# Decoding float64 weights in four passes in place of six, and moving three pairs of them to another stage

## The chip, the cores and the metric

The kernel runs on one core of a Trainium2 chip. The metric is device time in microseconds (us) of one execution; lower is better. TensorE does the matmuls, VectorE, ScalarE and GpSimd the elementwise work, and SyncE's queue issues nearly all DMAs. In rows of the profile these are PE (PEld is its weight load), DVE, ACT, POOL and SP.

## The reference

Three steps follow one another. First causal attention with a decay, for 4 batches x 8 heads, 576 positions, head size 64:

```python
scores = scale * (q @ k.T)
decay = cum[:, :, :, None] - cum[:, :, None, :]      # cum = cumsum(log(clip(f)))
attn = softmax(where(causal, -1e9, scores + decay))
x = (attn @ v) rearranged to [2304, 512]
h = x @ w_in                                         # 512 -> 2048
x = (h * sigmoid(h)) @ w_out                         # 2048 -> 512
out = ((x @ w_a) * (x @ w_b)) @ w_out2               # 512 -> 1536 -> 512
```

The weights `w_in`, `w_out`, `w_a`, `w_b`, `w_out2` arrive as float64, and the kernel has to make float32 numbers of them itself.

## The kernel before

**Stages.** In order of time: attention by pairs of heads (to about 183 us of the profiled span); the first in stage, `stage_in(0, ...)` (to about 361); the first out stage, `out_first` (to about 562), which begins with a part D of eight steps; the second in stage, `stage_in(1, ...)` (to about 827); the second out stage, `out_pairs`. Every matrix product is done by a Strassen-Winograd scheme: seven products of half-size blocks, on sums and differences of blocks that are called forms. Each float32 operand is split in a rounded part and a remainder (`split`: ScalarE casts, VectorE or GpSimd subtracts), and each product is three matmul passes. An in stage is a list `seq` of jobs (unit `u` of the weights, group `g` of tokens), seven products each.

**Weights.** They lie in 68 pieces of 128 x 512 numbers: 16 for the first in stage, 16 for its out stage (`F1`), 24 and 12 for the second. `decode(piece, ...)` fetches one piece (512 KB of float64) into a tile `raw` and makes float32 of it (L662 to L689). `load_unit` decodes the two pieces of one unit and makes the forms and their splits in one of three weight tiles `wA`, `wB`, `wC`. `load_piece` does the same for a piece of the first out stage, writes the decoded piece to DRAM (`wdram`) as well, and splits it into the tiles of `upper(v)`, two pieces for each of the eight `v`. `load_sums` later fetches the pair from `wdram` (`load_quarters`, into a tile of the tag `raw`) and makes the sums and differences that the other groups of tokens need. `decode_out(1, n)` decodes the 12 pieces of the second out stage during the second in stage and sends them to `wdram`.

**Tiles.** `raw`, `m` and `e` have two tiles each; tiles of one tag are given out in the order in which the program names them. Before the change the decoded piece is the tile `e`, and it is held until the unit's splits have read it; `raw` and `m` are free again at the end of the decoding.

**Order.** Nothing waits in a hand-written order. The class `Plan` simulates the engines with a cost for each operation, and at every step takes the ready operation that can start first; among those within 30 ns the one with the lowest priority number (`pr`, for most operations 1000 plus the planned time in us). An operation that may go to two engines (`either`: GpSimd or VectorE) gets the one that would end first. The order that comes out is each engine's program.

Of the kernel before, what the change touches and what calls it, by code (L numbers as in the profile page):

```python
# [9 lines left out]
F32 = mybir.dt.float32  # L10
F32R = mybir.dt.float32r
U32 = mybir.dt.uint32
BF16 = mybir.dt.bfloat16
AF = mybir.ActivationFunctionType
ALU = mybir.AluOpType
# [3 lines left out]
P = 128  # L19
# [20 lines left out]
PIECE = 512  # L40
# [4 lines left out]
UP = 5  # L45
# [179 lines left out]
def piece_of(stage, part):  # L225

    firsts = 2 * U1 + F1
    return {(0, "in"): 0, (0, "out"): 2 * U1, (1, "in"): firsts, (1, "out"): firsts + 2 * U2}[stage, part]
# [3 lines left out]
def model_kernel(ctx: ExitStack, tc: tile.TileContext, qk, q0, v, f, w, out):  # L232
# [44 lines left out]
    def buf(pool, tag, shape, dtype, name):  # L277
        n = SLOTS[tag]
        return Buf(tags[tag], lambda: (pools[tag] if pool is None else pool).tile(shape, dtype, name=name, tag=tag, bufs=n))
# [320 lines left out]
    def act(n, fn, reads, writes, prio):  # L600
        plan.add("ACT", 190 + n / 1.2, fn, reads, writes, prio)
# [2 lines left out]
        plan.add("DVE", 100 + n / 0.88 if sbuf else 165 + n / 0.96, lambda: fn(nc.vector), reads, writes, prio, port=sbuf)  # L604

    def pool(n, fn, reads, writes, prio):
        plan.add("POOL", 240 + 2.2 * n, lambda: fn(nc.gpsimd), reads, writes, prio)

    def either(n, fn, reads, writes, prio):
        plan.add("POOL", 240 + 2.2 * n, lambda: fn(nc.gpsimd), reads, writes, prio,  # L610
                 also=[("DVE", 100 + n / 0.88, lambda: fn(nc.vector))], port=True)

    def ss(n, fn, reads, writes, prio):
# [47 lines left out]
    def decode(piece, after, pr, single=False):  # L661

        n = PIECE
        if single:
            all_ = buf(zp, "z", [P, 3 * n], F32, f"raw_{piece}")
            raw, m, e = ((all_, i) for i in range(3))
            u = {raw: lambda: all_()[:, :2 * n].bitcast(U32), m: lambda: all_()[:, 2 * n:].bitcast(U32),
                 e: lambda: all_()[:, :2 * n].bitcast(U32).rearrange("p (c t) -> p c t", t=2)[:, :, 1]}
            ek = [e]
        else:  # L670
            raw = buf(dcp, "raw", [P, 2 * n], F32, f"raw_{piece}")
            m, e = (buf(dcp, t, [P, n], F32, f"{t}_{piece}") for t in "me")
            u = {t: lambda t=t: t().bitcast(U32) for t in (raw, m, e)}
            ek = [(e, 0), (e, 1)]
        src = w[piece * P * n:(piece + 1) * P * n].rearrange("(p c) -> p c", p=P)
        f = lambda t: u[t]().bitcast(F32)
        low, high = ((lambda k=k: u[raw]().rearrange("p (c t) -> p c t", t=2)[:, :, k]) for k in range(2))
        plan.dma(480, 8 * P * n, lambda: nc.sync.dma_start(u[raw](), src.bitcast(U32)), after, [raw], pr)
        act(n, lambda: nc.scalar.activation(f(m), high().bitcast(F32), AF.Copy, scale=2.0 ** -112), [raw], [m], pr)  # L679
        plan.add("DVE", 420, lambda: nc.vector.tensor_scalar(u[m](), u[m](), 3, None, ALU.logical_shift_left), (), [m], pr, port=True)  # L680
        plan.add("DVE", 690, lambda: nc.vector.scalar_tensor_tensor(  # L681
            u[m](), high(), 0x80000000, u[m](), ALU.bitwise_and, ALU.bitwise_or), [raw], [m], pr, port=True)
        plan.add("DVE", 600 if single else 420, lambda: nc.vector.tensor_scalar(u[e](), u[m](), 0xFF800000, None, ALU.bitwise_and), [m], ek + [raw] * single, pr, port=True)
        plan.add("DVE", 690, lambda: nc.vector.scalar_tensor_tensor(f(e), low(), 2.0 ** -52, f(e), ALU.mult, ALU.mult), [raw], ek, pr, port=True)  # L684
        if single:
            pool(n, lambda g: g.tensor_add(f(m), f(m), f(e)), ek, [m], pr)
            return m, lambda: f(m)
        pool(n, lambda g: g.tensor_add(e(), m(), e()), [m], ek, pr)  # L688
        return e  # L689

    def load_unit(stage, n, pr, after=()):

# [149 lines left out]
    def upper(v):  # L842

        t, n = (wouts[0][0], v) if v < UP else (wouts[0][1], v - UP)
        return t, lambda: t()[:, n * 2048:(n + 1) * 2048].rearrange("p (i f c) -> p i f c", i=2, f=4)
# [19 lines left out]
    def split_keys(n, hi, lo, val, reads, keys, pr):  # L865

        act(n, lambda: nc.scalar.copy(hi(), val()), reads, [k + (0,) for k in keys], pr)
        either(n, lambda e: e.tensor_sub(lo(), val(), hi().bitcast(F32)), list(reads) + [k + (0,) for k in keys], [k + (1,) for k in keys], pr)

    def load_piece(n, p):  # L870

        v, j = n // 2, n % 2
        t, w = upper(v)
        e = decode(piece_of(0, "out") + n, (), p)
        ek = [(e, 0), (e, 1)]
        plan.dma(480, 4 * P * PIECE, lambda: nc.sync.dma_start(wdram[0][n], e()), ek, [("w", 0, n)], p)
        split_keys(4 * P, lambda: w()[:, 0, 2 * j:2 * j + 2], lambda: w()[:, 1, 2 * j:2 * j + 2], lambda: e().rearrange("p (i c) -> p i c", i=2), ek,
                   [(t, v, 2 * j), (t, v, 2 * j + 1)], p)

    def load_sums(v, p, q):  # L880

        t, w = upper(v)
        low, x = lower(v)
        m, keys, combine = load_quarters(0, v, p)
        e = buf(dcp, "e", [P, 2, 2 * P], F32, f"s_{v}")
        for i, (a, b) in enumerate(((1, 3), (2, 0))):
            either(2 * P, lambda g, i=i, a=a, b=b: g.tensor_add(e()[:, i], m()[:, a], m()[:, b]), [keys[a], keys[b]], [(e, i)], p)
        split_keys(4 * P, lambda: w()[:, 0, 1:3], lambda: w()[:, 1, 1:3], e, [(e, 0), (e, 1)], [(t, v, 1), (t, v, 2)], p)
        combine(1, 1, 0, False, q)
        combine(2, 3, 2, False, q)  # L890
        combine(0, 0, 3, True, q)
        split(4 * P, lambda: x()[:, 0, :2], lambda: x()[:, 1, :2], lambda: m()[:, 1:3], keys[1:3], (low, "n", v, 0), q, either)
        split(2 * P, lambda: x()[:, 0, 2:], lambda: x()[:, 1, 2:], lambda: m()[:, :1], keys[:1], (low, "n", v, 1), q, either)

    def decode_out(stage, n, pr):

        key, m = decode(piece_of(stage, "out") + n, (), pr, True)
        plan.dma(480, 4 * P * PIECE, lambda: nc.sync.dma_start(wdram[stage][n], m()), [key], [("w", stage, n)], pr)

    def load_pairs(h, slot, pr):  # L900

# [279 lines left out]
    GROUPS = (4,), (3,), (2,), (1, 0)  # L1181

    LOW = 10
    LEAVE, SPOTS = (30, 14), ((0, 1, 2, 3), (0, 1, 3), (1, 3))

    for pair in range(NH // 2):
# [64 lines left out]
    seq = by((0, 1, 2)) + each((3, 4)) + by((5, 6, 7))  # L1251
    place = lambda u, g: t + seq.index((u, g)) * T_JOB
    end = t + len(seq) * T_JOB
    hooks = {(u - 3, 2): [U(0, u, place(u, 0) - 20, [(heads['nm', 15], 8)] if u == 3 else ())] for u in range(3, U1)}
    pair_us = 8 * T_PROD / 1000
    EARLY = lambda n: max(-30 + 3 * n, n // 2 * pair_us - 16) if n < 2 * UP else n // 2 * pair_us - 14
    hooks[5, 1] = [open_first] + [lambda n=n, p=1000 + end + EARLY(n): load_piece(n, p) for n in range(F1)]
    t = stage_in(0, U1, seq, hooks, t)

    def then(part, g, t):  # L1260
# [79 lines left out]
```

## Time and profile before

| | |
|---|---|
| median of 3 runs | 971.04 us (970.42 to 973.73) |
| the profiled execution | 968.52 us, span 966.8 us |
| TensorE clock granted over the span | 0.997 |
| HBM read, written | 124.73 MB, 66.84 MB |

The span is the time from the first to the last instruction of the profiled execution. An engine's busy time counts its instructions, not its waits. Matmuls overlap each other, so a busy TensorE is one that has a matmul under way, and a stretch in which its busy time is short of the stretch is one in which it waited.

### The profile page before, as it was taken

How to read it: one execution, taken by the hardware profiler on the slowest of the kernel's cores; microseconds unless marked ns; L12 is line 12 of the kernel's file. 1: busy time of each engine (PE TensorE's matmuls, PEld its weight loads, DVE VectorE, ACT ScalarE, POOL GpSimd, SP SyncE). 2: the span in 40 equal slices, each digit the busy share in tenths (PEclk: the TensorE clock that was granted, in tenths of full speed). 3: DMA queues.
4: the chain of work that ended last, by engine and by line, in shares of the span. 5: the costliest groups of instructions: out<-in, count | busy, mean ns of one | idle time of the engine just before them, and what ended most of it. 6: DMA issues, size and time to landing. Idle time of an engine off the chain costs nothing.

```text
span 966.8 us, 16788 instructions
## 1 busy us (share of the span) xinstructions
PE 934.3 (97%) x5892; PEld 874.8 (90%) x5892; DVE 814.7 (84%) x1397; ACT 531.6 (55%) x1116; POOL 530.1 (55%) x443
## 2 busy tenths in 40 slices
PE   8999999999999999999999889999999999899998
PEld 7666666899999999998899779999999999899998
DVE  7878997875888998878889999999879978988774
ACT  6888879954565654455455443343433334453642
POOL 5667885012787564479434776677888867400000
PEclk9999999999999999999999999999999999999999
DMA  5553433144565899876789405365554425896861
GB/s 155 181 171 137 152 121 111 58 167 172 213 229 195 293 335 357 283 234 238 248 282 333 135 1 196 150 217 184 183 204 163 169 103 197 267 346 237 266 224 66
DMA packets 78261, 192.69 MB, mean 199 GB/s; under 512 B 10972, under 2 KB 36716, under 8 KB 78144
## 3 DMA queue, kind: packets, MB, share of 16 engines
q1 hardware_dynamic: 78064, 191.17, 56.5%
q8 instruction: 46, 0.75, 0.3%
q10 hardware_dynamic: 112, 0.45, 0.2%
q14 instruction: 39, 0.32, 0.1%
HBM read 124.73 MB, written 66.84 MB: 198 GB/s over the span
## 4 chain that ended last, share of the span: by engine, by line
PE 62%; DVE 14%; POOL 9%; DMA 7%; issue 4%; ACT 3%; SPq 1%; DVEq 0%; POOLq 0%; ACTq 0%
PE a L734 17%; PE m L1075 13%; PE b L734 8%; PE d L927 6%; PE g L734 4%; PE s L452 4%; PE pv L574 3%; POOL m L861 2%; DVE z L638 2%; DMA raw<-in_w 2%; POOL e L708 2%; PE t_x L528 2%; POOL w L619 1%; PE t_y L528 1%; POOL wo L619 1%
## 5 line engine op out<-in xcount | busy, mean ns | idle before, releaser
L734 PE MATMUL a<-x,w 128*128 128x384 f32 x960 | 185.2, 335 | 0.8 <-ACT c L784 0.6
L734 PEld LDWEIGHTS a<-x,w 128*128 128x128 f32 x960 | 167.7, 188 | 2.1 <-ACT c L784 0.9
L688 POOL TENSOR_TENSOR e<-m,e 128x512 f32<-128x512 f32 x56 | 87.9, 1579 | 129.4 <-DVE e L684 125.2
L619 POOL TENSOR_TENSOR w<-e,w 128x512 fp32r<-128x512 f32 x80 | 104.6, 1318 | 45.9 <-ACT w L618 40.7
L734 PE MATMUL b<-x,w 128*128 128x384 f32 x480 | 96.8, 335 | 3.7 <-DVE c L802 1.9
L734 PEld LDWEIGHTS b<-x,w 128*128 128x128 f32 x480 | 84.1, 188 | 5.0 <-POOL w L619 2.2
L618 ACT CAST w<-e 128x512 fp32r<-128x512 f32 x80 | 44.9, 569 | 51.8 <-POOL e L708 29.9
L486 ACT ACTIVATE p<-p,nm 128x512 f32<-128x512 f32 (+3 forms) x128 | 70.7, 561 | 4.2 <-DVE nm L478 4.1
L734 PE MATMUL a<-xb,w 128*128 128x384 f32 x360 | 71.3, 335 | 0.7 <-ACT c L792 0.6
L1075 PE MATMUL m<-morea,wo 128*128 128x384 f32 x378 | 68.1, 334 | 0.6 <-DVE morea L619 0.6
L1075 PEld LDWEIGHTS m<-morea,wo 128*128 128x128 f32 x378 | 65.7, 188 | 0.9 <-DVE morea L619 0.9
L734 PEld LDWEIGHTS a<-xb,w 128*128 128x128 f32 x360 | 63.1, 188 | 1.3 <-ACT c L792 0.9
L478 DVE CUSTOM_DVE_ANT_0 p<-s,maskw 128x512 f32<-128x512 f32 (+3 forms) x128 | 56.3, 483 | 8.8 <-PE t_x L528 3.4
L404 POOL TENSOR_TENSOR qkl<-qk,qkh 128x304 fp32r<-128x304 f32 x60 | 53.3, 915 | 17.8 <-DVE qkh L396 17.4
L784 ACT COPY c<-a 128x384 f32<-128x384 f32 x60 | 28.5, 477 | 51.9 <-PE a L734 33.9
L681 DVE SCALAR_TENSOR_TENSOR m<-raw,m 128x512 uint32<-128x512 uint32 x56 | 49.8, 896 | 0.6
L734 PE MATMUL g<-x,w 128*128 128x384 f32 x240 | 48.3, 335 | 1.4 <-DVE c L823 0.8
L789 ACT COPY c<-b 128x384 f32<-128x384 f32 x60 | 28.7, 478 | 37.6 <-PE b L734 36.7
L680 DVE TENSOR_SCALAR m<-m 128x512 uint32<-128x512 uint32 x56 | 40.6, 729 | 9.7 <-ACT m L679 8.4
L684 DVE SCALAR_TENSOR_TENSOR e<-raw,e 128x512 f32<-128x512 uint32 x56 | 48.5, 883 | 0.2
L792 ACT COPY c<-a 128x384 f32<-128x384 f32 x60 | 28.7, 479 | 35.5 <-PE a L734 35.2
L734 PE MATMUL b<-xa,w 128*128 128x384 f32 x240 | 48.0, 334 | 0.0
(237 smaller groups left out, 2466.4 us busy)
## 6 DMA issues: line engine op xcount, KB each, us to landing
raw<-in_w SPq DMA_DIRECT2D x68, 512.0 KB
cdram<-z SPq DMA_DIRECT2D x36, 576.0 KB
g<-gdram SPq DMA_DIRECT2D x24, 768.0 KB
c_False<-cdram SPq DMA_DIRECT2D x36, 384.0 KB
c_True<-cdram SPq DMA_DIRECT2D x36, 384.0 KB
gdram<-z SPq DMA_DIRECT2D x32, 384.0 KB
h<-gdram SPq DMA_DIRECT2D x16, 576.0 KB
qk<-in_qk SPq DMA_DIRECT2D x15, 608.0 KB
```

Of the source, the lines that this page charges most:

```text
L404: plan.add("POOL", t_pool(QK // 4), lambda c=c: nc.gpsimd.tensor_sub(lo()[:, c], raw()[:, c], hi().bitcast(F32)[:, c]), [(hi, "h"), raw], ...
L478: plan.add("DVE", t_dve(nj) + 82, lambda out=out, low=low, o=o, mk=mk: nc.vector.tensor_tensor_reduce(out(), o(), mk, -SCALE, 3.0e38, ALU. ...
L486: plan.add("ACT", t_act(sum(IB[ib]), 279), lambda b=b, c=c, nj=sum(IB[ib]): nc.scalar.activation(b()[:, :nj], b()[:, :nj], AF.Exp, bias=nm ...
L618: act(n, lambda: nc.scalar.copy(hi(), val()), reads, [key + (0,)], pr)
L619: eng(n, lambda e: e.tensor_sub(lo(), val(), hi().bitcast(F32)), list(reads) + [key + (0,)], [key + (1,)], pr)
L680: plan.add("DVE", 420, lambda: nc.vector.tensor_scalar(u[m](), u[m](), 3, None, ALU.logical_shift_left), (), [m], pr, port=True)
L681: plan.add("DVE", 690, lambda: nc.vector.scalar_tensor_tensor(u[m](), high(), 0x80000000, u[m](), ALU.bitwise_and, ALU.bitwise_or), [raw], ...
L684: plan.add("DVE", 690, lambda: nc.vector.scalar_tensor_tensor(f(e), low(), 2.0 ** -52, f(e), ALU.mult, ALU.mult), [raw], ek, pr, port=True)
L688: pool(n, lambda g: g.tensor_add(e(), m(), e()), [m], ek, pr)
L734: nc.tensor.matmul(ps()[:, :HB], a, b, start=start and k == 0 and i == 0, stop=k == 1 and i == 2, skip_group_check=not start)
L927: nc.tensor.matmul(ps[o]()[:, :HB], a, b, start=start and i == 0, stop=stop and i == 2, skip_group_check=not fresh)
L1075: nc.tensor.matmul(ps[o]()[:, :HB], a, b, start=start and i == 0, stop=stop and i == 2, skip_group_check=not fresh)
```

## The change

Decoding takes other passes. Before, for each piece: ScalarE makes a float from the high word (exponent moved, sign and 20 bits of the mantissa); VectorE shifts it, puts the sign in, cuts out the power of two into `e`, and multiplies the low word by it; GpSimd adds the two. After: ScalarE makes the float as before, and in a second pass makes an integer of 0 to 7 out of the upper 16 bits of the low word and writes it over the lower 16 bits of the high word; VectorE shifts and sets three bits in one pass, and brings sign and those three bits in with a second. GpSimd has no part, and the tile `e` isn't used: the decoded piece is `m`.

The pieces 10 to 15 of the first out stage (three pairs, `v` = 5 to 7) are decoded by `decode_out(0, n)` during the first in stage, one at each of the jobs 1 to 6, and go to `wdram`. Their `upper` tiles are then filled by `load_upper`, which fetches the pair with `load_quarters` and only splits it. For the in stage, units 4 to 6 may be loaded with an earlier priority (`place(u - 3, 2) + T_JOB`, where that is earlier). The planner's cost of a GpSimd operation of `n` elements is 250 + 2.65 n ns in place of 240 + 2.2 n.

```diff
     def pool(n, fn, reads, writes, prio):
-        plan.add("POOL", 240 + 2.2 * n, lambda: fn(nc.gpsimd), reads, writes, prio)
+        plan.add("POOL", 250 + 2.65 * n, lambda: fn(nc.gpsimd), reads, writes, prio)
     def either(n, fn, reads, writes, prio):
-        plan.add("POOL", 240 + 2.2 * n, lambda: fn(nc.gpsimd), reads, writes, prio,
+        plan.add("POOL", 250 + 2.65 * n, lambda: fn(nc.gpsimd), reads, writes, prio,
                  also=[("DVE", 100 + n / 0.88, lambda: fn(nc.vector))], port=True)
...
-        act(n, lambda: nc.scalar.activation(f(m), high().bitcast(F32), AF.Copy, scale=2.0 ** -112), [raw], [m], pr)
-        plan.add("DVE", 420, lambda: nc.vector.tensor_scalar(u[m](), u[m](), 3, None, ALU.logical_shift_left), (), [m], pr, port=True)
+        high = lambda: words().rearrange("p (c t) -> p c t", t=2)[:, :, 1]
+        short = lambda k: words().bitcast(U16).rearrange("p (c t) -> p c t", t=4)[:, :, k]
+        bits = lambda: val().bitcast(U32)
+        act(n, lambda: nc.scalar.activation(val(), high().bitcast(F32), AF.Copy, scale=2.0 ** -112), [raw], keys, pr)
+        act(n, lambda: nc.scalar.activation(short(2), short(1), AF.Relu, bias=7.0, scale=-2.0 ** -13), [], [raw], pr)
+        plan.add("DVE", 420, lambda: nc.vector.tensor_scalar(bits(), bits(), 3, 7, ALU.logical_shift_left, ALU.bitwise_or), (), keys, pr, port=True)
         plan.add("DVE", 690, lambda: nc.vector.scalar_tensor_tensor(
-            u[m](), high(), 0x80000000, u[m](), ALU.bitwise_and, ALU.bitwise_or), [raw], [m], pr, port=True)
-        plan.add("DVE", 600 if single else 420, lambda: nc.vector.tensor_scalar(u[e](), u[m](), 0xFF800000, None, ALU.bitwise_and), [m], ek + [raw] * single, pr, port=True)
-        plan.add("DVE", 690, lambda: nc.vector.scalar_tensor_tensor(f(e), low(), 2.0 ** -52, f(e), ALU.mult, ALU.mult), [raw], ek, pr, port=True)
-        if single:
-            pool(n, lambda g: g.tensor_add(f(m), f(m), f(e)), ek, [m], pr)
-            return m, lambda: f(m)
-        pool(n, lambda g: g.tensor_add(e(), m(), e()), [m], ek, pr)
-        return e
+            bits(), high(), 0x80000007, bits(), ALU.bitwise_and, ALU.bitwise_xor), [raw], keys, pr, port=True)
+        return (m, val) if single else m
...
+    def load_upper(v, p):
+        t, w = upper(v)
+        m, keys, _ = load_quarters(0, v, p)
+        for j in range(0, 4, 2):
+            split_keys(4 * P, lambda j=j: w()[:, 0, j:j + 2], lambda j=j: w()[:, 1, j:j + 2], lambda j=j: m()[:, j:j + 2], keys[j:j + 2],
+                       [(t, v, j), (t, v, j + 1)], p)
...
     def decode_out(stage, n, pr):
-        key, m = decode(piece_of(stage, "out") + n, (), pr, True)
-        plan.dma(480, 4 * P * PIECE, lambda: nc.sync.dma_start(wdram[stage][n], m()), [key], [("w", stage, n)], pr)
+        if stage:
+            m, val = decode(piece_of(stage, "out") + n, (), pr, True)
+            keys = [m]
+        else:
+            m = val = decode(piece_of(stage, "out") + n, (), pr)
+            keys = [(m, 0), (m, 1)]
+        plan.dma(480, 4 * P * PIECE, lambda: nc.sync.dma_start(wdram[stage][n], val()), keys, [("w", stage, n)], pr)
...
+    PRE, EARLIER = 1, 20
...
-    hooks = {(u - 3, 2): [U(0, u, place(u, 0) - 20, [(heads['nm', 15], 8)] if u == 3 else ())] for u in range(3, U1)}
+    hooks = {(u - 3, 2): [U(0, u, min(place(u, 0) - EARLIER, place(u - 3, 2) + T_JOB), [(heads['nm', 15], 8)] if u == 3 else ())] for u in range(3, U1)}
...
-    hooks[5, 1] = [open_first] + [lambda n=n, p=1000 + end + EARLY(n): load_piece(n, p) for n in range(F1)]
+    hooks[5, 1] = [open_first] + [lambda n=n, p=1000 + end + EARLY(n): load_piece(n, p) for n in range(2 * UP)]
+    hooks[5, 1] += [lambda v=v, p=1000 + end + EARLY(2 * v): load_upper(v, p) for v in range(UP, U1)]
+    for k, n in enumerate(range(2 * UP, F1)):
+        hooks.setdefault(seq[PRE + k], []).append(lambda n=n, p=1000 + t + (PRE + k) * T_JOB: decode_out(0, n, p))
```

## Rows read from the trace of the kernel before

**Rows 1.** The page, busy time of each engine, share of the span, instructions.
```profile
PE 934.3 (97%) x5892; PEld 874.8 (90%) x5892; DVE 814.7 (84%) x1397; ACT 531.6 (55%) x1116; POOL 530.1 (55%) x443
```

**Rows 2.** Busy time by stretch (us from the start): length, engines, clock, DMA, GB/s.
```profile
20.00:183.00 163.00, 161.08 (x1410) 113.68 (x1408) 136.80 (x453) 143.28 (x405) 104.94 (x100) 1.00 0.41 137
183.00:361.00 178.00, 175.16 (x1001) 172.30 (x996) 147.62 (x200) 104.44 (x220) 93.59 (x71) 1.00 0.60 219
420.00:430.00 10.00, 8.47 (x48) 7.83 (x47) 8.31 (x10) 5.87 (x14) 8.60 (x9) 1.00 0.59 191
450.00:466.00 16.00, 11.62 (x60) 9.82 (x59) 13.67 (x13) 8.79 (x15) 15.71 (x14) 1.00 0.57 186
525.00:565.00 40.00, 32.25 (x170) 30.04 (x169) 37.93 (x41) 18.03 (x30) 28.13 (x18) 0.96 0.40 129
565.00:585.00 20.00, 18.04 (x103) 17.40 (x102) 18.87 (x18) 10.12 (x18) 14.63 (x10) 1.00 0.00 1
585.00:750.00 165.00, 165.00 (x954) 165.00 (x953) 147.66 (x242) 64.90 (x127) 123.43 (x102) 1.00 0.53 191
765.00:770.00 5.00, 3.10 (x19) 2.78 (x18) 4.99 (x11) 0.96 (x2) 3.54 (x3) 1.00 0.53 182
827.00:834.00 7.00, 4.43 (x25) 3.79 (x24) 7.00 (x8) 2.05 (x4) 4.14 (x3) 1.00 0.67 220
```

**Rows 3.** Groups by line and shape: line, engine, operation; busy us, mean ns.
```profile
L688 POOL TENSOR_TENSOR e<-m,e 128x512 f32<-128x512 f32 x56 | 87.9, 1579 | 129.4 <-DVE e L684 125.2 <-ACT hl_C L618 2.6 <-PE b L734 1.0
L684 DVE SCALAR_TENSOR_TENSOR e<-raw,e 128x512 f32<-128x512 uint32 x56 | 48.5, 883 | 0.2
L683 DVE TENSOR_SCALAR e<-m 128x512 uint32<-128x512 uint32 x56 | 34.2, 627 | 1.8 <-POOL w L619 1.2
L679 ACT ACTIVATE m<-raw 128x512 f32<-128x512 f32 x56 | 37.5, 676 | 15.9 <-DMA raw<-in_w 15.1 <-DVE z L835 0.6
L486 ACT ACTIVATE p<-p,nm 128x512 f32<-128x512 f32 x32 | 23.2, 729 | 3.5 <-DVE nm L478 3.5
```

**Rows 4.** Operations on the tile e: duration ns min/median/max, first and last start.
```profile
L683 DVE TENSOR_SCALAR e<-m x56: 408/418/2067, 39.7 to 765.0; 128x512 uint32<-128x512 uint32 x56
```

**Rows 5.** The chain that ended last, in order of time: start us, us, what.
```profile
57.42 2.85 PE pv L574 x24
67.55 2.85 PE pv L574 x24
...
88.44 2.85 PE pv L574 x24
...
299.38 2.75 POOL w L619 x2
...
456.98 3.31 POOL m L861 x3
...
765.44 1.20 DVE e L684 x2
```

**Rows 6.** SP's queue in order of time, around 410 us.
```profile
410.48 0.37 SPq L856 DMA_DIRECT2D m<-wdram  x1
```

**Rows 7.** Instructions in order of time around 540 us, on VectorE, GpSimd and TensorE.
```profile
536.72 3.50 DVE L683 TENSOR_SCALAR e<-m 128x512 uint32<-128x512 uint32 x2
540.14 2.88 DVE L684 SCALAR_TENSOR_TENSOR e<-raw,e 128x512 f32<-128x512 uint32 x2
542.95 3.56 DVE L619 TENSOR_TENSOR hl_C<-h,hl_C 128x384 fp32r<-128x384 f32 x2
...
535.94 2.01 POOL L619 TENSOR_TENSOR w<-e,w 128x512 fp32r<-128x512 f32 x1
542.50 3.19 POOL L688 TENSOR_TENSOR e<-m,e 128x512 f32<-128x512 f32 x2 [0.63 <-DVE e L684]
...
544.61 5.06 PE L927 MATMUL f<-hl_C,wo 128*128 128x384 f32 x17 [4.36 <-DVE hl_C L619]
```

**Rows 8.** The line of the Silu: the load of its activation table, ns.
```profile
L768 ACT ACT_TABLE_LOAD  x1: 1283/1283/1283, 187.1 to 187.1; - x1
```

More of the change, by code (lines that the diff above doesn't have):

```diff
@@ L12 @@
 U32 = mybir.dt.uint32
+U16 = mybir.dt.uint16
 BF16 = mybir.dt.bfloat16
@@ L665, in decode @@
             all_ = buf(zp, "z", [P, 3 * n], F32, f"raw_{piece}")
[L666 to L669, printed above, removed]
+            raw, m = ((all_, i) for i in range(2))
+            words, val = (lambda: all_()[:, :2 * n].bitcast(U32)), (lambda: all_()[:, 2 * n:])
@@ L670, in decode @@
         else:
             raw = buf(dcp, "raw", [P, 2 * n], F32, f"raw_{piece}")
-            m, e = (buf(dcp, t, [P, n], F32, f"{t}_{piece}") for t in "me")
-            u = {t: lambda t=t: t().bitcast(U32) for t in (raw, m, e)}
-            ek = [(e, 0), (e, 1)]
+            m = buf(dcp, "m", [P, n], F32, f"m_{piece}")
+            words, val = (lambda: raw().bitcast(U32)), (lambda: m())
+        keys = [m] if single else [(m, 0), (m, 1)]
         src = w[piece * P * n:(piece + 1) * P * n].rearrange("(p c) -> p c", p=P)
-        f = lambda t: u[t]().bitcast(F32)
@@ L677, in decode @@
-        low, high = ((lambda k=k: u[raw]().rearrange("p (c t) -> p c t", t=2)[:, :, k]) for k in range(2))
-        plan.dma(480, 8 * P * n, lambda: nc.sync.dma_start(u[raw](), src.bitcast(U32)), after, [raw], pr)
-        act(n, lambda: nc.scalar.activation(f(m), high().bitcast(F32), AF.Copy, scale=2.0 ** -112), [raw], [m], pr)
-        plan.add("DVE", 420, lambda: nc.vector.tensor_scalar(u[m](), u[m](), 3, None, ALU.logical_shift_left), (), [m], pr, port=True)
-        plan.add("DVE", 690, lambda: nc.vector.scalar_tensor_tensor(
-            u[m](), high(), 0x80000000, u[m](), ALU.bitwise_and, ALU.bitwise_or), [raw], [m], pr, port=True)
@@ L689, in decode @@
-        return e
+        high = lambda: words().rearrange("p (c t) -> p c t", t=2)[:, :, 1]
+        short = lambda k: words().bitcast(U16).rearrange("p (c t) -> p c t", t=4)[:, :, k]
+        bits = lambda: val().bitcast(U32)
+        plan.dma(480, 8 * P * n, lambda: nc.sync.dma_start(words(), src.bitcast(U32)), after, [raw], pr)
+        act(n, lambda: nc.scalar.activation(val(), high().bitcast(F32), AF.Copy, scale=2.0 ** -112), [raw], keys, pr)
+        act(n, lambda: nc.scalar.activation(short(2), short(1), AF.Relu, bias=7.0, scale=-2.0 ** -13), [], [raw], pr)
```

## The prediction

> **What bounds the kernel now.** I read the page's first part, then the busy time by stretch, then the chain of waits, and only then the groups. TensorE is busy for 97% of the span, VectorE for 84%, ScalarE and GpSimd for 55% each [rows 1]. So the removal of work from VectorE and GpSimd pays only where TensorE waits for that work. Those places are few [rows 2]. In the long middle of the second in stage (585 to 750) TensorE is busy in every microsecond, although VectorE is at 89%: there nothing can be won. The reader is to see how much shorter TensorE's busy time is than its stretch: 1.9 us in attention (20 to 183), 2.8 in the first in stage, 1.5 in 420 to 430, 4.4 in 450 to 466, 7.8 in 525 to 565, 2.0 in 565 to 585, 1.9 in 765 to 770 and 2.6 in 827 to 834. In 525 to 565 the granted clock is 0.96 as well; 4% of 40 us is another 1.6. Together 26.5 us. Attention hides a little more, because overlapping matmuls count as busy there: the chain has the pv product of successive pairs at 57.42 and 67.55, 10.13 apart, and two pairs later than 67.55 it stands at 88.44, which is 0.63 more than twice 10.13 [rows 5].
>
> **What the passes cost.** For each of 68 pieces two VectorE passes go, of 0.627 and 0.883 us in the mean, and one GpSimd pass of 1.579 [rows 3] (the rows are those of 56 pieces; I take the 12 others at the same means). That is 68 x 1.510 = 102.7 us off VectorE, which comes to some 712, and 68 x 1.579 = 107.4 off GpSimd, to some 423. ScalarE gets one more pass of 128 x 512. No row shows one that reads and writes two bytes in each eight. The nearest rows are the Copy of the high words, 0.676, and an Exp of 512 columns that like the new pass has a bias, 0.729 [rows 3]. I take 0.729; from below 0.676, from above twice 0.729, 1.46, as an estimate for the case that strided half words go at half the rate. So 49.6 us (46 to 99), and ScalarE comes to some 581 of 967: idle enough, except in attention, where it is busy for 143.3 of 163 us [rows 2].
>
> The two passes that VectorE keeps change only a constant and an operator; I cost that at nothing, and if the shift with a second operator fell from the 0.408 that it can reach now [rows 4] to the other pass's 0.883, 68 x 0.475 = 32 us of the 103 would be lost again.
>
> On one piece alone the work behind a free tile hardly gets shorter. Before: cut out, multiply, add, 0.627 + 0.883 + 1.579 = 3.1 us. After: Copy, Relu, shift, merge, 0.676 + 0.729 + 0.627 + 0.883 = 2.9. The reason is that the decoded piece now stays in `m`, so the Copy and the shift, which ran ahead while `e` was held, have to wait until the splits of the unit before are done. What is gained is engine time, not the time to the piece.
>
> A pass of 512 columns takes 0.676 on ScalarE and 0.408 at best on VectorE [rows 3, 4]. The Trainium skill (ScalarE: Activation LUTs, Rules for kernel authors) says that relu, multiply and add belong on VectorE and not on ScalarE, which speaks against this change. By it the pass would be 0.3 us shorter and would sit on the engine that is at 84%; the row bears out the duration, but the sum goes by who has time, and there ScalarE is the better place.
>
> **Stretch by stretch.**
>
> *Attention, three units.* In 67.55 to 88.44 the slip of 0.63 stands beside decode passes of VectorE. For three units I take 1.0 gained (0 to 1.9). Against it stand six new Relu passes, and the Copies and Relus of pieces 10 to 15, as far as they are put into attention: they have no transfer to wait for, and the planner fills any hole. All 18 passes are 6 x 0.729 + 6 x (0.676 + 0.729) = 12.8 us, ScalarE's holes 19.7. The loss lies between 0 and 12.8; I take 0.5, near the lower end, since the six Copies that already lie there leave TensorE only 1.9 us of waiting. Behind a ScalarE pass its Exps and copies of transposes are queued, and TensorE's next pv waits for these. Net 0.5.
>
> *First in stage.* Units 5 to 7 come just in time through GpSimd: the chain runs over its splits (299.38) [rows 5]. Each unit loses 2 x 1.579 = 3.2 us there. Of the 2.8 us I take 1.3 (-1 to 2.8): the first jobs get six pieces of decoding more, where GpSimd has nothing to do, and piece 15 stands between units 3 and 4 in the order of tiles.
>
> *420 to 466.* The sums for the other groups are made from `wdram`. Their tiles have the tag `raw`, in the order named, so the first fetch is issued only at 410.48 [rows 6], when the decoding of the 16 pieces has given its last tile but one, though part D begins at 361. Then eight `v` are crammed into 45 us; GpSimd is busy for 15.7 of 16, and the chain is its combines (456.98) [rows 2, 5]. After the change six decodings leave this place (6 x 1.579 = 9.5 us of GpSimd, 6 x 1.51 = 9.1 of VectorE, at the least), three fetches of 512 KB take the place of six fetches and three of the tiles are not asked for, so the sums start earlier. Of 1.5 + 4.4 = 5.9 us I take 4.3 (0 to 5.9).
>
> *525 to 585.* VectorE is busy for 37.9 of 40 us. TensorE waits 4.36 us for `hl_C`, which stands behind two cut-outs and two multiplications, 6.3 us, and is itself slowed to 3.56 beside the GpSimd adds [rows 7]. One would like to book all of it. But `m` comes free only with the split that ends at 537.95, so shift and merge of the same two pieces go to this very place. What leaves is the 3.19 us of adds and with it part of the stretching of VectorE's passes (0.408 to 2.067) [rows 4, 7]. I take 2.5 of 11.3 us (-4 to 8; the loss if the Copies stand in ScalarE's queue behind a cast that waits for TensorE, so that unit 1 of the second in stage is late next).
>
> *765 to 770.* The last unit is held up by the multiplications at 765.44 [rows 5], after two adds and the splits on a GpSimd that is nearly full. Of 1.9 I take 1.8 (0 to 1.9).
>
> *827 to 834.* The second out stage's weights and first operands; no decoding is left by then. 0 (-1 to 2).
>
> The planner's new GpSimd cost reorders what goes to either engine all over the kernel. I price it at nothing, hidden under TensorE's busy time wherever there is some; its bounds are in those of 525 to 585.
>
> Sum: 0.5 + 1.3 + 4.3 + 2.5 + 1.8 = 10.4. The profiled execution took 968.5, so 958.1 for its like; it lies 2.5 under the median of the runs, 971.0, so 960.6 as a median, which is what I predict.
>
> **The rivals.**
>
> *Crowding stays.* Decoding keeps its place beside the casts of `hl_C`, nothing is gained in 525 to 585 and half of the rest: 5 us, 966. For it: the tile argument above. Against it: GpSimd's adds really go.
>
> *All of it.* Each wait in which a decode pass or a full GpSimd has a share goes to its upper bound: 1.9 + 2.8 + 5.9 + 8 + 1.9 = 20.5, 950.5. For it: VectorE has little air in every one of these stretches and gets 13% of its work taken off.
>
> *Nothing.* The waits are set by transfers and forms that stay, and each stretch finds another last wait: 968 to 971. Against it: 765.44 is a removed pass.
>
> *Slower, through ScalarE in attention.* The half-word pass is slow and the six early pieces are pushed into the holes. At 1.46 the passes are 6 x 1.46 + 6 x 2.14 = 21.6 us, more than the 19.7 of holes. The other stretches give 10.4 - 0.5 = 9.9; so it is slower by over 0.3% when more than 9.9 + 2.9 = 12.8 us of delay reach TensorE; with all 21.6 it is 971.0 - 9.9 + 21.6 = 983. For it: 88% busy; against it: no sign that columns cost ScalarE more for their stride (0.676 for the strided Copy against 0.729 for the dense Exp).
>
> The same place would suffer if the Relu needed another activation table than Exp: a load takes 1.283 us [rows 8], two for each of 12 Relus are 31 us, 971 - 10 + 31 = 992. The Trainium skill (ScalarE: Activation LUTs, Table sets: the hidden batching unit) states that cheap functions like relu are in every set; by it this can't happen, and no Relu stands in the trace of before to show it.
>
> **How the numbers follow.** Forecast (955 to 966) 0.50, crowding stays 0.14, all of it 0.16, nothing 0.10, slower by slow passes 0.08, by table loads 0.02. 0.3%, about what a measurement of this kernel can tell from no change, is 2.9 us, so faster means under 968.1: 0.50 + 0.14 + 0.16 = 0.80; same 0.10; slower 0.10. The range takes the forecast, the crowding, most of "all of it" and half of "nothing": 949 to 970.
>
> **What would show it.** The Relu's mean near 0.73, and no more table loads than before. VectorE's busy time near 712, GpSimd's near 423, ScalarE's near 581. The first fetch from `wdram` well before 410 and TensorE nearly full from 420 to 466. No wait of 1.9 us before the last unit of the second in stage. Attention's end within 1 us of 183. In 525 to 585 still the largest single wait, shorter than 4.4. The prediction is wrong if attention ends later by more than 3 us, or if the sums in the first out stage start no earlier than before.

## The result and the profile after

The changed kernel takes 959.78 us in the median (959.04 to 960.96, 4 runs), the kernel before 970.73 beside it; the ratio is 0.9882, with a 95% interval of 0.9859 to 0.9905. That is 11 us faster, within 1 us of the forecast of 960.6. The total came out; two terms of the sum did not, and their errors cancelled.

The profiled execution took 959.04 us, its span is 957.3. First the page's line of busy times, to be set beside [rows 1].

```profile
PE 931.6 (97%) x5892; PEld 875.3 (91%) x5892; DVE 702.2 (73%) x1293; ACT 610.7 (64%) x1186; POOL 369.3 (39%) x341
```

VectorE lost 112.5 us of work and GpSimd 160.8, more than the removed passes (102.7 and 107.4): GpSimd issues 102 instructions fewer, 68 of them the adds; the planner's new cost gives it less of what may go to either engine (24 instructions fewer with that cost alone, e7 below). ScalarE gained 79 us, not 50.

The busy time by stretch, first the stretches of [rows 2] with the same limits, then attention and the first in stage with the limits that they have now. Columns as in [rows 2].

```profile
420.00:430.00 10.00, 10.00 (x60) 10.00 (x59) 9.12 (x12) 6.07 (x14) 5.85 (x7) 1.00 0.65 211
450.00:466.00 16.00, 16.00 (x95) 16.00 (x94) 11.26 (x17) 9.18 (x14) 0.00 (x0) 1.00 0.80 283
525.00:565.00 40.00, 34.47 (x192) 33.12 (x193) 38.09 (x40) 24.15 (x37) 30.99 (x16) 1.00 0.32 103
565.00:585.00 20.00, 17.20 (x96) 16.34 (x97) 17.20 (x25) 10.42 (x18) 15.20 (x13) 1.00 0.36 130
765.00:770.00 5.00, 5.00 (x31) 5.00 (x30) 2.59 (x5) 1.58 (x3) 1.29 (x1) 1.00 0.29 118
...
20.00:190.00 170.00, 164.33 (x1424) 115.56 (x1425) 132.72 (x453) 156.38 (x419) 90.89 (x91) 1.00 0.45 145
190.00:360.00 170.00, 167.85 (x971) 166.66 (x967) 114.71 (x176) 126.83 (x240) 48.95 (x45) 1.00 0.65 233
```

In 420 to 430 and in 450 to 466 TensorE no longer waits, and GpSimd, 15.7 of 16 us busy before, does nothing at all in the second of them. Between 525 and 585 it still waits, 5.5 + 2.8 us in place of 7.8 + 2.0, and the clock is whole there (0.96 before). The clock had fallen in the ten microseconds with the longest wait of that place, to 0.83, a mean of its two levels, 1.2 and 2.4 GHz; in the kernel before:

```profile
540.00:550.00 10.00, 5.50 (x22) 4.74 (x21) 9.52 (x10) 1.86 (x4) 5.07 (x3) 0.83 0.50 165
```

The wait at 765 is gone. But in attention TensorE waits for 5.7 us where it waited for 1.9.

Busy time hides part of a wait, so the stages are better measured by where TensorE stands. These are the lines of the last pv product, of the first products of part D and of the last products of the first out stage; the two numbers ahead of the semicolon are first and last start. First the kernel before, then the changed one.

```profile
L574 PE MATMUL pv<-th,vt x384: 219/379/591, 25.6 to 182.9; 128*64 128x448 f32 x64, 128*64 128x320 f32 x32, 128*64 128x192 f32 x32, 128*64 128x64 f32 x32
L927 PE MATMUL d<-wo_1b,wo x96: 334/334/444, 355.0 to 400.6; 128*128 128x384 f32 x96
L927 PE MATMUL f<-hl_B,wo x120: 334/334/445, 440.4 to 562.3; 128*128 128x384 f32 x120
```

```profile
L575 PE MATMUL pv<-th,vt x384: 219/379/591, 26.8 to 190.1; 128*64 128x448 f32 x64, 128*64 128x320 f32 x32, 128*64 128x192 f32 x32, 128*64 128x64 f32 x32
L935 PE MATMUL d<-wo_1b,wo x96: 334/334/334, 359.9 to 404.5; 128*128 128x384 f32 x96
L935 PE MATMUL f<-hl_B,wo x120: 333/334/444, 442.1 to 554.2; 128*128 128x384 f32 x120
```

So the last pv product stands 7.2 us later, and part D begins 4.9 us later. From there to the end of the first out stage it took 207.3 us and takes 194.3, 13.0 less. From there to the span's end it is 404.5 and 403.1. The sum of 4.9 - 13.0 - 1.4 is -9.5: the span is shorter by that. A single place is less sure than the span: the changed kernel and e1 below have the same order and passes of the same length, and their first pv products start at 26.8 and 25.6, their parts D at 359.9 and 361.4.

Most of the 13.0 lies ahead of the last 40 us of that stage. In the kernel before, and then in the changed one:

```profile
355.00:522.00 167.00, 160.30 (x912) 157.54 (x912) 144.28 (x164) 82.28 (x133) 88.94 (x64) 1.00 0.82 283
```

```profile
360.00:518.00 158.00, 158.00 (x914) 158.00 (x913) 118.97 (x139) 83.99 (x130) 49.23 (x38) 1.00 0.78 279
```

The same products take 9 us less, and TensorE no longer waits among them.

What became slow is one instruction, in the groups by line and shape of the changed kernel.

```profile
L680 ACT ACTIVATE raw<-raw 128x512 uint16<-128x512 uint16 x68 | 91.1, 1388 | 0.6
L679 ACT ACTIVATE m<-raw 128x512 f32<-128x512 f32 x56 | 36.2, 674 | 6.0 <-DMA raw<-in_w 5.0 <-POOL w L620 1.0
```

The Relu takes 1.388 us, twice the Copy beside it. The chain of waits of the changed kernel passes through it in attention:

```profile
42.01 0.47 ACT th L534
42.48 2.41 ACT raw L680 x2
44.89 0.91 ACT th L534 x2
45.80 0.05 issue
45.84 0.98 PE t_y L529 x7
```

Two Relus in a row hold up two copies of transposes (`th`) for 2.41 us, and TensorE's next transposes start when these are done.

### The profile page after: what moved, and what is told of

It reads as the page before. It is cut to its first block, busy times and chain, and to the rows that moved or that the text cites. A ratio compares the mean times of both kernels' runs of the same rounds, so it can differ in the third digit from the quotient of the medians.

```text
span 957.3 us, 16537 instructions
## 1 busy us (share of the span) xinstructions
PE 931.6 (97%) x5892; PEld 875.3 (91%) x5892; DVE 702.2 (73%) x1293; ACT 610.7 (64%) x1186; POOL 369.3 (39%) x341
## 4 chain that ended last, share of the span: by engine, by line
PE 79%; ACT 7%; DVE 5%; issue 4%; DMA 2%; POOL 2%; SPq 1%; DVEq 0%; ACTq 0%; POOLq 0%
PE a L729 22%; PE m L1083 13%; PE b L729 11%; PE f L935 10%; PE d L935 7%; PE g L729 6%; PE s L453 3%; PE pv L575 2%; ACT raw L680 1%; PE t_y L529 1%; ACT p L487 1%; PE t_x L529 1%; ACT th L534 1%; DMA rb<-invs 1%; POOL w L620 1%
## 5 line engine op out<-in xcount | busy, mean ns | idle before, releaser
L620 POOL TENSOR_TENSOR w<-m,w 128x512 fp32r<-128x512 f32 x80 | 99.7, 1255 | 206.7 <-ACT w L619 206.7
L680 ACT ACTIVATE raw<-raw 128x512 uint16<-128x512 uint16 x68 | 91.1, 1388 | 0.6
L619 ACT CAST w<-m 128x512 fp32r<-128x512 f32 x80 | 44.1, 571 | 32.9 <-POOL m L703 21.6
L682 DVE SCALAR_TENSOR_TENSOR m<-raw,m 128x512 uint32<-128x512 uint32 x56 | 45.0, 808 | 18.0 <-ACT raw L680 17.6
L802 DVE TENSOR_TENSOR d<-a,c 128x384 f32<-128x384 f32 x60 | 33.7, 561 | 28.8 <-PE a L729 27.6
L575 PE MATMUL pv<-th,vt 128*64 128x448 f32 (+4 forms) x384 | 46.8, 393 | 0.0
```

Source lines behind the costliest of these rows:

```text
L575: nc.tensor.matmul(ps()[p * D:(p + 1) * D, o0:o0 + w_].rearrange("d (u c) -> d u c", c=D), vt()[:, jb, p], src, start=n == 0, stop=last)
L619: act(n, lambda: nc.scalar.copy(hi(), val()), reads, [key + (0,)], pr)
L620: eng(n, lambda e: e.tensor_sub(lo(), val(), hi().bitcast(F32)), list(reads) + [key + (0,)], [key + (1,)], pr)
L680: act(n, lambda: nc.scalar.activation(short(2), short(1), AF.Relu, bias=7.0, scale=-2.0 ** -13), [], [raw], pr)
L802: dve(HB, lambda e: e.tensor_add(pd(), pa(), pc(2)), [a, (c, 2)], [d], at(4) - 3)
```

## The experiments

All ran beside the kernel before on the same chip; the times are medians. The diffs are shortened, with `...` for what is left out. In a diff, lines with - are those of the changed kernel, unless it says otherwise.

**Which side of the Relu is slow, and what does it cost?** Three kernels with the changed kernel's order on every engine; only the Relu's operands differ. `low` stands for the low words as 4-byte numbers.

```diff
-nc.scalar.activation(short(2), short(1), AF.Relu, bias=7.0, scale=-2.0 ** -13)
+nc.scalar.activation(short(2), low, AF.Relu, bias=7.0, scale=-2.0 ** -29)      # e1
+nc.scalar.activation(low, short(1), AF.Relu, bias=7.0, scale=-2.0 ** -13)      # e2
+nc.scalar.activation(low, low, AF.Relu, bias=7.0, scale=-2.0 ** -29)           # e3
```

> The Relu reads the whole low word (4 bytes) and still writes the half word; the integer it makes is the same, and the order on every engine is that of the changed kernel. Theory A (the pass takes 1.39 us because of its two-byte access, and attention's end, 190.1 in place of 182.9, is mostly due to that): if the read is what costs, the Relu falls to 0.73, nine Relus before 190 us save 5.9 us of ScalarE, the last pv product comes near 185 and the time to 954 to 956. If the write costs, the Relu stays at 1.39 and the time at 959.8. Theory B (attention is late because of the three early pieces and the new order, however long the Relu is): even at 0.73 the last pv product stays within 2 us of 190 and the time above 957.5.

> The Relu reads the half word and writes a whole word, over the low word; the three low bits of a weight are then not those of the reference, which leaves out their part of the result. Same order. Theory A with the write as the cause: the Relu at 0.73 and the last pv product near 185. With the read as the cause: 1.39 and 190. Theory B: 190 in either case.

> The Relu reads and writes whole words (low word to low word); the three low bits of the weights are left out of the result. Same order. Theory A, whichever side costs: the Relu at 0.73, the last pv product near 185, the time 954 to 956. If only both sides together make it slow, this is the run that shows it against the two others. Theory B: the last pv product within 2 us of 190, the time above 957.5.

Measured: e1 959.99 us (ratio 0.9875, 0.9859 to 0.9892), e2 952.83 in its only run, e3 953.04 (0.981, 0.9796 to 0.9825). The line of the Relu in the groups, first of e1:

```profile
L680 ACT ACTIVATE raw<-raw 128x512 uint16<-128x512 uint32 x68 | 91.2, 1388 | 0.6
```

and of e2:

```profile
L680 ACT ACTIVATE raw<-raw 128x512 uint32<-128x512 uint16 x68 | 44.6, 676 | 0.0
```

Reading two bytes in eight costs nothing (0.676, the price of the Copy); writing two bytes in eight doubles the pass. And the doubling costs 7 us of the whole (e1 against e3): in e2 the last pv product starts at 185.8 and part D at 353.2, against 190.1 and 359.9, and from part D on e2 keeps the changed kernel's pace: to the last `f` product it is 193.9 us against 194.3. Theory A holds, B falls. A's times, 954 to 956, were too long, and the pv product came back by less than A had expected (187.3 in e3, not 185); but D, which all of attention and the first in stage stand before, came back by 5.2 to 6.7. So the long Relu costs some 3 to 4 us by the end of attention and the rest in the first in stage.

**Without the Relu**, the order otherwise kept:

```diff
-act(n, lambda: nc.scalar.activation(short(2), short(1), AF.Relu, bias=7.0, scale=-2.0 ** -13), [], [raw], pr)
+act(n, lambda: None, [], [raw], pr)
```

> The changed kernel without the Relu, its order otherwise kept; the three low bits of the weights are left out of the result. It gives the whole price of the pass. Theory A (what hurts is ScalarE's time in attention): a second halving gives less than the first, since a pass of 0.68 fits better in the holes: last pv product 183 to 185, 949 to 952. Rival G: the pass costs by standing there at all, each time a fixed wait in the chain of a piece, and its removal gives as much again as its halving: 945 to 947.

Measured: 952.41 us (0.9813, 0.9791 to 0.9835); last pv product 186.1, part D 353.5. The pass of 0.68 costs nothing that can be told from none at all; all of the 7 us lies in the second half of the 1.39. Theory A holds, and G's 945 to 947 is far off. A's numbers (183 to 185 for the pv product, 949 to 952) were missed, the second narrowly: some 3 us of the shift from 182.9 are not the Relu's. About half of them is one wait of TensorE, here in this run:

```profile
142.49 3.74 DVE L645 CAST x<-z 128x768 fp32r<-128x768 f32 x2
146.15 0.54 DVE L535 COPY th<-t_x 128x384 f32<-128x384 f32 x1
146.75 0.44 PE L529 MATMUL t_x<-ident,p 128*128 128x128 f32 x2 [1.65 <-DVE th L535]
```

A copy of transposes stands on VectorE behind two casts for the first in stage. This wait, 1.6 or 1.7 us, is in every run that has the changed kernel's order, with a long Relu, a short one or none (the changed kernel, e1, e2, e3, e9, e10), and not in the kernel before: it belongs to the order. The rest stays open. By part D, which is 1.5 earlier than before the change, the 3 us are given back.

**The early pieces kept out of attention.**

```diff
-    m = val = decode(piece_of(stage, "out") + n, (), pr)
+    m = val = decode(piece_of(stage, "out") + n, [(heads['nm', 15], 8)], pr)
```

> Pieces 10 to 15 wait until attention's last row maximum, as unit 3 does, so that none of their passes stands in attention; the rest is the changed kernel, with the slow Relu. Theory A: six Relus of 1.39 stay in attention, three with three Copies leave it: 3 x 2.06 = 6.2 us off ScalarE; the last pv product 185 to 188, and what is gained is given back partly at the first jobs (959 +- 2). Theory B: the last pv product back at 183 to 184, the time 953 to 955.

Measured: 959.58 us (0.9876, 0.9861 to 0.9891), last pv product 188.4, part D 361.0. The last pv product is 1.7 us earlier, part D is not. The pv product is a fraction of a microsecond outside A's 185 to 188, the time is A's (959 +- 2); B's 183 to 184 is far off. What stays in attention are the six Relus of the units. The planner made the order anew here, so the 1.7 can't be put down to the early pieces alone.

**The new passes without the early pieces**, and **the early pieces with the old passes**. The first:

```diff
-hooks[5, 1] = [open_first] + [... load_piece(n, p) for n in range(2 * UP)]
-hooks[5, 1] += [... load_upper(v, p) for v in range(UP, U1)]
-for k, n in enumerate(range(2 * UP, F1)):
-    hooks.setdefault(seq[PRE + k], []).append(... decode_out(0, n, p))
+hooks[5, 1] = [open_first] + [... load_piece(n, p) for n in range(F1)]
```

> The changed kernel without the early pieces: all 16 pieces of the first out stage are decoded where they were before, by the new passes, slow Relu included. Theory C (the waits of 420 to 466 us went because six decodings left that place; the shorter passes took those of the second in stage's beginning and end): some 5 us of waiting come back there, attention ends 2 us earlier, 961 to 963. Theory D (the shorter passes alone empty 420 to 466, and the early pieces only cost time in attention): 955 to 958.

The first keeps the planner's new cost and the units' earlier priorities. The second is the kernel before (its lines are those with -) with `load_upper`, the changed `decode_out` and these lines put in:

```diff
-hooks[5, 1] = [open_first] + [... load_piece(n, p) for n in range(F1)]
+hooks[5, 1] = [open_first] + [... load_piece(n, p) for n in range(2 * UP)]
+hooks[5, 1] += [... load_upper(v, p) for v in range(UP, U1)]
+for k, n in enumerate(range(2 * UP, F1)):
+    hooks.setdefault(seq[1 + k], []).append(... decode_out(0, n, p))
```

> The kernel before with the early pieces and the loading from DRAM alone: old passes, old priorities of the units, old planner cost. Theory C: 420 to 466 is emptied of its waits (7 us of lost pace), attention loses 1 to 2 us by three pieces' passes: 965 to 967. Theory D: the old passes keep GpSimd and VectorE full there, and attention's loss remains: 970 to 973.

Measured: 959.34 us without the early pieces (0.9894, 0.988 to 0.9909), 965.22 with them alone (0.9949, 0.9929 to 0.9969). From the first D product to the last `f` product: 207.3 us before, 195.8 with the passes and no early pieces (359.0 to 554.8), 200.7 with the early pieces alone (357.7 to 558.4), 194.3 with both. The gains don't add: 11.5, 6.6, together 13.0. The early pieces give 5.2 us to the kernel before (970.42 beside it) and nothing that can be told from noise to one that has the new passes. The first run's time lies between C's (961 to 963) and D's (955 to 958); its stretch says D, for the passes alone empty it nearly. The second run's time is C's. The stretch behind part D shows it; here in the kernel before and with the early pieces alone:

```profile
430.00:470.00 40.00, 35.62 (x198) 33.82 (x197) 35.57 (x34) 24.95 (x44) 36.79 (x32) 1.00 0.67 222
```

```profile
430.00:470.00 40.00, 37.60 (x217) 37.13 (x216) 36.59 (x44) 21.87 (x36) 23.23 (x20) 1.00 0.79 274
```

here without the early pieces:

```profile
430.00:470.00 40.00, 38.72 (x223) 38.36 (x222) 39.26 (x46) 27.15 (x42) 22.82 (x20) 1.00 0.77 262
```

and here in the changed kernel:

```profile
430.00:470.00 40.00, 40.00 (x233) 40.00 (x232) 31.48 (x39) 24.98 (x36) 9.09 (x8) 1.00 0.87 308
```

Of 4.4 us of waiting the early pieces alone leave 2.4, the new passes 1.3, both together nothing. Without the early pieces 1.3 us come back, not 5; VectorE is nearly full there (39.3 of 40 us), but just in time. That the early pieces alone gain less in the whole stage may have a second reason: behind a wait the granted clock is 0.70 in 540 to 550 there, where it is 0.83 in the kernel before.

**The planner's cost of GpSimd alone**, in the kernel before:

```diff
-240 + 2.2 * n
+250 + 2.65 * n
```

> The kernel before with nothing but the planner's new cost of a GpSimd operation. By theory C the new order gives nothing that can be told from noise: 968 to 974. The rival, that the better cost is a good part of the gain (more to VectorE where GpSimd is the later one), gives 963 to 967.

Measured: 970.51 us (0.9998, 0.9987 to 1.001). It gives nothing to the time by itself. But it moves the places inside the span, without any other pass:

```profile
L574 PE MATMUL pv<-th,vt x384: 219/379/591, 26.7 to 185.0; 128*64 128x448 f32 x64, 128*64 128x320 f32 x32, 128*64 128x192 f32 x32, 128*64 128x64 f32 x32
L927 PE MATMUL d<-wo_1b,wo x96: 334/334/334, 352.8 to 397.3; 128*128 128x384 f32 x96
```

The last pv product is 2.1 us later than in the kernel before and part D 2.2 earlier. So between two kernels whose order the planner made anew, a difference of 2 us at one place can't be put down to a pass. The units' earlier priorities were tried in no run by themselves.

**The planner told of the long Relu:**

```diff
-act(n, lambda: nc.scalar.activation(short(2), short(1), ...), [], [raw], pr)
+plan.add("ACT", 1390, lambda: nc.scalar.activation(short(2), short(1), ...), [], [raw], pr)
```

> The changed kernel with 1390 ns as the planner's cost of the Relu, in place of 617: same passes, another order. Theory A: ScalarE's work in attention is the same, so the last pv product stays at 187 to 191; 957 to 962. The rival (attention is late because the planner, believing in 617, puts the passes where there is no room): last pv product 183 to 186, 953 to 956.

Measured: 959.13 us (0.9872, 0.9854 to 0.9889), last pv product 186.2, part D 357.7. The time is A's; the pv product lies just above the rival's 183 to 186: attention gets 3.9 us of its delay back, D only 2.2, and the total can't be told from the changed kernel's. Both are partly right, and a better cost doesn't free ScalarE.

**Can the short Relu be had with the whole result?** Then the integer lies in a word of its own, and a third pass of two inputs has to bring it in. Three ways were tried. In e8 VectorE's shift takes it along:

```diff
-nc.scalar.activation(short(2), short(1), AF.Relu, bias=7.0, scale=-2.0 ** -13)
+nc.scalar.activation(low, short(1), AF.Relu, bias=-0.5, scale=2.0 ** -13)
...
-plan.add("DVE", 420, ... tensor_scalar(bits(), bits(), 3, 7, ALU.logical_shift_left, ALU.bitwise_or)
+plan.add("DVE", 690, ... scalar_tensor_tensor(bits(), bits(), 3, low, ALU.logical_shift_left, ALU.bitwise_xor)
...
-    bits(), high(), 0x80000007, bits(), ALU.bitwise_and, ALU.bitwise_xor)
+    bits(), high(), 0x80000000, bits(), ALU.bitwise_and, ALU.bitwise_xor)
```

> A version after the first four runs: the Relu takes the half word and writes a whole word over the low word (the integer itself, cut off and not rounded, so a weight may differ in its last bit); VectorE shifts and brings the integer in with one pass of two inputs, and the sign with another. ScalarE should have 68 x 0.71 = 48 us less than the changed kernel, VectorE 68 x 0.26 = 18 more. If the half-word write was the whole of the trouble: Relu 0.68, last pv product near 186, 952 to 954. The rival: the shift as a pass of two inputs costs back in the crowded stretch around 540 us what attention gains, 956 to 959.

Measured: 964.12 us (0.9941, 0.9922 to 0.9961). The rival's side, and worse than it. Two things had changed, the passes and, through their costs, the order. So e9 keeps the changed kernel's order and adds one VectorE pass in the place of the merge:

```diff
-nc.scalar.activation(short(2), short(1), ...)
+nc.scalar.activation(low, short(1), ...)
...
-lambda: nc.vector.scalar_tensor_tensor(bits(), high(), 0x80000007, bits(), ALU.bitwise_and, ALU.bitwise_xor)
+lambda: [nc.vector.scalar_tensor_tensor(bits(), a, k, bits(), ALU.bitwise_and, ALU.bitwise_xor)
+         for a, k in ((low, 7), (high(), 0x80000000))]
```

> Why was the version with whole words, 964.1, slower than the changed kernel, when the same short Relu with the changed kernel's own order gave 952.8? Theory E: the planner's order, which came out otherwise because the first VectorE pass was given 690 in place of 420 ns. Theory F: VectorE's longer work. Here the planner's costs and so the order of every engine are those of the changed kernel; the Relu writes its integer (rounded as there) as a whole word over the low word, and VectorE has one pass more for each piece, 68 x 0.69 = 47 us, in the place of the merge. The result is that of the changed kernel. E: Relu 0.68, attention as in the runs with short Relus (last pv product near 186 to 187), 953 to 957. F: 960 to 965, with the loss between 525 and 585 us.

Measured: 964.49 us (0.9927, 0.9909 to 0.9945); VectorE 751.6 us busy. Against e3, with the same order and the same short Relu, 11.4 us are lost to 68 VectorE passes. F holds, but only a part of the loss is where it had put it: part D begins at 361.1 in place of 354.7, so over half of it is lost before; from there to the last `f` product 4.2 us more than in e3 (198.1 against 193.9). In 525 to 585 TensorE is busy for 50.8 of 60 us, in e3 for 51.8, and its granted clock is 0.94 there, in e3 1.00: together some 4.6 us. The pv product is at 190.1 again, although ScalarE is relieved: in attention VectorE's passes are as dear here as ScalarE's.

In e12 GpSimd brings the integer in:

```diff
-nc.scalar.activation(short(2), short(1), ...)
+nc.scalar.activation(low, short(1), ...)
...
-    bits(), high(), 0x80000007, bits(), ALU.bitwise_and, ALU.bitwise_xor), [raw], keys, pr, port=True)
+    bits(), high(), 0x80000000, bits(), ALU.bitwise_and, ALU.bitwise_xor), [raw], keys, pr, port=True)
+pool(n, lambda g: g.tensor_tensor(bits(), bits(), low, op=ALU.subtract), [raw], keys, pr)
```

> Which engine's relief brought the gain? The Relu writes whole words (0.68), VectorE shifts and merges the sign as in the changed kernel, and GpSimd brings the three bits in with a last pass of two inputs (an exact 32-bit subtraction), 68 x 1.3 to 1.6 us, where before it had its add. The result is that of the changed kernel; the planner makes its own order. Theory H (the gain is VectorE's 103 us; GpSimd's 107 were mostly idle room): last pv product near 186, waits of 420 to 466 still gone, 952 to 957, faster than both kernels. Theory I (GpSimd's adds, which stretch VectorE's passes and end the chain of a unit, were a good part): the waits before the last unit of the second in stage and around 450 come back, 960 to 966.

Measured: 966.44 us (0.995, 0.9932 to 0.9967). H falls by its time, 952 to 957, though its two signs came true: the last pv product is at 186.4, and from 420 to 470 TensorE does not wait. I's time, 960 to 966, is missed narrowly, and of I's two places neither the one before the last unit nor the one around 450 came back. The loss stands before part D, which begins at 361.9 (354.7 in e3). What came back is in the waits of TensorE between 190 and 600 us (engine and line, waited for: us in total, times, longest):

```profile
PE a L730 <- POOL w L620: 3.9, 2, 3.2
...
PE b L730 <- POOL w L620: 1.8, 2, 1.0
```

TensorE waits for units whose splits GpSimd does, 5.7 us, in the changed kernel 2.1, and between 300 and 320 the granted clock is 0.76 and 0.90, which is some 3 us more. The order is the planner's own, so what is the passes' and what the order's is not parted here. None of the versions with a third pass beats the changed kernel.

## Why the prediction was right, point by point

**What bounds the kernel: right.** VectorE and GpSimd lost 273 us of work, and the time fell by 11, at the places where TensorE had waited for them. In 585 to 750, where there was no wait, nothing was won.

**The signs.** Of what the prediction had asked for, these came: no more table loads than before, the fetches from DRAM well before 410, TensorE full from 420 to 466, no wait before the last unit, and a largest wait in 525 to 585 shorter than 4.4 (2.1). These did not: the Relu near 0.73, attention's end within 1 us of 183, and GpSimd's and ScalarE's busy times near 423 and 581. And one of the two things that were to show the prediction wrong happened: attention ends later by more than 3 us. So the time came out, and the step on attention failed.

**The Relu's price: the term that was mis-sized.** I took 0.729, from the nearest rows, with 1.46 as the bound from above; it is 1.388, because of the half words that it writes. The nearest rows had neither a two-byte read nor a two-byte write; the read turned out to cost nothing. With the slow write the premise of the slower rival nearly came true, the half-word pass at 1.46 in attention. Its price did not: of 21.6 us of delay, the length of all 18 passes, 7 came about, and only some 3 to 4 of them by the end of attention. Of the six early pieces only three came to stand in attention (nine Relus of 1.388 stand there). That the rest of these passes fell into ScalarE's holes is the likely reason; it was not shown pass by pass.

**Attention and the first in stage:** forecast 0.5 + 1.3 = 1.8 us faster to the first product of D, measured 4.9 slower. With the Relu at 0.676, the only thing that differs from the changed kernel, it is 1.8 faster in e2 (353.2 against 355.0) and 0.3 faster in e3 (354.7). So for a pass of that length the forecast is not contradicted. But it is not borne out as it was argued either: the planner's cost alone, priced at nothing, brings part D to 352.8 with all the old passes (e7). What the removed adds give in the first in stage was not measured apart from the order.

**420 to 466 and 525 to 585:** forecast 4.3 + 2.5, measured 13.0 over the whole of the first out stage. In 420 to 466 the bound from above was reached: all 5.9 us of waiting are gone. From the start of D to 522 it is 6.7 us of waiting and 9 of time, so the waits hide some 2 us more than the busy time tells. The argument was that six decodings leave that place. It works in part (6.6 us in e6), but it was not needed: the shorter passes without them give 11.5 (e5). That the two don't add was not seen. In 525 to 585 the number holds: 9.7 us of waiting became 8.3, and the 1.6 of the fallen clock went, 3.0 against 2.5, over half of it the clock's. The argument on the tile `m` can be read off the timeline there, VectorE's first and then TensorE's:

```profile
534.26 4.72 DVE L620 TENSOR_TENSOR hl_C<-h,hl_C 128x384 fp32r<-128x384 f32 x2
538.90 0.75 DVE L681 TENSOR_SCALAR m<-m 128x512 uint32<-128x512 uint32 x2
539.58 2.92 DVE L682 SCALAR_TENSOR_TENSOR m<-raw,m 128x512 uint32<-128x512 uint32 x2
542.42 1.41 DVE L620 TENSOR_TENSOR hl_B<-h,hl_B 128x384 fp32r<-128x384 f32 x2
...
534.39 2.20 PE L935 MATMUL f<-wo_1b,wo 128*128 128x384 f32 x11 [1.73 <-DVE wo_1b L620]
539.04 2.18 PE L935 MATMUL f<-hl_C,wo 128*128 128x384 f32 x11 [1.20 <-DVE hl_C L620]
543.02 3.24 PE L935 MATMUL f<-hl_B,wo 128*128 128x384 f32 x17 [1.62 <-DVE hl_B L620]
```

Shift and merge of unit 1 stand where cutting and multiplying stood [rows 7], only behind `hl_C` now and not ahead of it. TensorE waits 1.7 us for `wo_1b`, 1.2 for `hl_C` and 1.6 for `hl_B` there, 4.5 in all; before it was 4.4 for `hl_C` and then 2.3 for `hl_B`:

```profile
560.45 2.20 PE L927 MATMUL f<-hl_B,wo 128*128 128x384 f32 x11 [2.29 <-DVE hl_B L619]
```

**765 to 770:** forecast 1.8, all 1.9 gone; right. **827 to 834:** forecast 0; of 2.6 us of waiting there 1.7 are left, ten microseconds earlier, so 0.8 was won.

**VectorE's kept passes:** costed at nothing, and right: the shift with its second operator takes 0.476 in the mean, where the shift of before took 0.729. That GpSimd, 161 us less busy, runs beside it less often would explain that; it was not tried by itself.

**The first fetch from DRAM:** forecast well before 410.48 [rows 6]. The upper tiles' come first; the sums' first fetch is then the fourth, 28 us earlier than before:

```profile
365.68 0.57 SPq L851 DMA_DIRECT2D m<-wdram  x1
...
382.43 0.37 SPq L851 DMA_DIRECT2D m<-wdram  x1
```

**The table loads:** no rival. Either kernel has three loads in all. The one at the Silu's line is again a single one, at 193.9 us, and the Relus, which stand on both sides of it (42.4 to 749.6), need none. The Trainium skill (ScalarE: Activation LUTs, Table sets: the hidden batching unit) says that relu is in every set; the trace agrees.

**The size of the sum.** In the spans' terms, 9.5 us measured against 10.4: up to part D it is 6.7 us worse than forecast (4.9 slower, not 1.8 faster), which is about the slow half of the Relu (7 us); in the first out stage it is 6.2 better (13.0, not 4.3 + 2.5), behind it 0.4 worse (1.4, not 1.8). That it came out within 1 us is luck in the first two, not in the rest.

## What to carry to other kernels

When a pass is priced by its nearest row, look for the one property that no row has (here: two-byte writes in steps of eight bytes), keep it as a bound, and measure it by changing that operand alone while the order stays. Two changes that empty the same wait don't add, so each has to be priced after the other is in. When a planner makes the order, run its new order with the old work too: here it moved places inside the span by 2 us and the whole by nothing. On a kernel whose TensorE is 97% busy, 68 passes moved the time by 7 us (ScalarE, the second 0.7 us of each Relu), 11 (VectorE, 0.73 each) and 13 (GpSimd, 1.5 each, in an order of its own), and by nothing for the first 0.7 us on ScalarE: an engine's busy share did not tell how much room it has at the places that set the end.

## What the runs showed of the hardware that was not expected

A ScalarE pass that writes two-byte numbers eight bytes apart takes twice as long: 1.388 us for 128 x 512, against 0.676 when the same pass writes four-byte numbers eight bytes apart; reading two bytes of each eight costs nothing (0.676, against 0.677 for four of each eight). Whether the two-byte size or its step does it was not tried. A 32-bit integer subtraction on GpSimd, 128 x 512, took 1.51 us in the mean of 56, about like its float add of before, 1.58 [rows 3].
